# A fused bias-attention and FFN kernel: weight halves staged at most five ahead, and narrow bias groups moved to a score bank

## The chip, the cores and the metric

The kernel runs on one core of one Trainium2 chip. The metric is the device time of one execution in microseconds (us). TensorE is called PE below, VectorE DVE, ScalarE ACT, GpSimd POOL and SyncE SP, as in the profile.

## The reference

Four batches, eight heads, 576 positions, head width 64. The bias of the scores comes from a small network on a ratio of logarithms of distances, the same for every batch. Attention is followed by a layer norm and an FFN of width 2048 with a residual sum.

```python
scores = scale * np.matmul(q, k.transpose(0, 1, 3, 2))
x = (psi_rel / psi_i)[..., None]          # log1p(|i-j|) / log1p(max(i,1))
h = np.maximum(x @ w1 + b1, 0.0)          # 1 -> 32
bias = h @ w2                             # 32 -> 8 heads
scores = scores + bias.transpose(2, 0, 1)[None, :, :, :]
...
attn = attn / (np.sum(attn, axis=-1, keepdims=True) + 1e-09)
x = np.matmul(attn, v)                    # heads concatenated to (4, 576, 512)
xn = (x - mu) / np.sqrt(var + 1e-06) * g_ln
ch = np.maximum(xn @ w_ch1, 0.0) @ w_ch2  # 512 -> 2048 -> 512
return x + ch
```

The FFN weights arrive as float64 bit patterns. The kernel decodes them to float32 itself, and then splits each into two float16 parts, so that every FFN product is made of three float16 products.

## The kernel before

**Units.** A unit u is one batch, one block of 128 rows (for the last 64 rows two heads share one unit) and one head: 144 units. A Python loop over steps u writes the program. Step u holds softmax1(u) (DVE L437 adds scores and bias and finds the minimum, ACT L441 takes the exponential), the loads, softmax2(u-1), staging and decoding of weights, one group of bias rows, at odd u the two score products qk(u+1) and qk(u+2) (PE L394), the product with V (PE L483 or L512), some pieces of FFN work (PE L712 and L741), and the splitting of decoded weights. A scheduler (the tile framework's, with its own model of time) then decides in which order each engine's instructions stand. On the chip each engine works through its list in that order, and semaphores make it wait where data or a buffer are missing.

**Weights.** There are 32 raw halves n = 2f + i of 512 KB each. load_w (L613) stages a half by a DMA on SP's queue (L630), into a weight slot that is not yet needed (`fit`); the last slots, called wend, serve several halves in turn. decode_w (L637) turns it into float32 by three DVE instructions (L646, L649, L651) and gives it to PE for a Gram product (L660). The Gram products of a group of weights accumulate in the PSUM bank y1, and give the group's scale (w_scale, L663). With it split_w (L680) makes the float16 parts on ACT (L686) and DVE (L689). Only then can the FFN use the weights. How far the staging may run ahead of the decoder is this line:

```python
            if not fit or n >= len(decoded) + (6 if ustep[0] < 9 else 10):
                return False
```

**Bias groups.** The 576 rows of the bias are made in 36 groups of 16. bias_relu (L154) makes the hidden layer on DVE (L163) and ACT (L161), bias_mm (L168) multiplies on PE into a PSUM tile bps (L202 for the first 12 groups, L182 for the later ones), ACT scales it into an SBUF tile ev (L188, two instructions, one for each side of the diagonal), and a DMA writes ev to a DRAM tensor nb (L215). Later each unit loads its bias tile ldb from there (L330, L332).

**PSUM.** Score tiles sps have the tag "s" in a pool of two buffers of two banks each, which qk takes in turn. The first 12 bias groups and the one wide group (more than 512 columns) use the same two buffers. The other 23 groups use the bank y1, which is free of Gram products by then. The bank y0 collects the second FFN product (L741), and DVE adds it to x (L752).

The order of the first blocks is tails of batches 0 and 1, then block 0; the groups of block 1 are made one per step from step 28 on, those of blocks 2 and 3 every third step.

Of the kernel before, what the change touches and what calls it, by code (L numbers as in the profile page):

```python
# [8 lines left out]
F32 = mybir.dt.float32  # L9
# [13 lines left out]
def kernel(  # L23
# [33 lines left out]
    ps_s = ctx.enter_context(tc.tile_pool(name="ps_s", bufs=2, space=bass.MemoryType.PSUM))  # L57
    ps_x = ctx.enter_context(tc.tile_pool(name="ps_x", bufs=1, space=bass.MemoryType.PSUM))
    ps_h = ctx.enter_context(tc.tile_pool(name="ps_h", bufs=1, space=bass.MemoryType.PSUM))
    ps_y = ctx.enter_context(tc.tile_pool(name="ps_y", bufs=1, space=bass.MemoryType.PSUM))  # L60
# [78 lines left out]
    def after(ins, dep):  # L139
        if dep is not None:  # L140
            tc.add_manual_dep(ins.ins, dep.ins.name,
                              mybir.DependencyInfo(mybir.DependencyClass.Sync,
                                                   mybir.DependencyReason.DATA),
                              reason="pace")

    def stage(gi, name, s=0):
        if gi in gorder[0:7] and name == "r" and s % 2:
            r = ptp.tile([128, 10, 128], F16, tag="pt", name="rp")
            return r.rearrange("p a b -> p (a b)").bitcast(F32)[:, 0:EW]
        if gi in gorder[0:12] and name == "r" and gi < 35:  # L150
            return e16p.tile([128, 1152], F16, tag="e16", name="rh").bitcast(F32)
        return ep.tile([128, EW], F32, tag="e", name=name)
# [15 lines left out]
    def bias_mm(gi):  # L168
        rs, ndve = rt.pop(gi)
        nrev = 16 * gi + 16  # L170
        ntot = nrev + SEQ - 16 * gi
        n = max(SEQ - 16 * gi, nrev + 1)
        if gi in gorder[12:] and n <= 512:
            ps = ps_y.tile([128, 512], F32, tag="y1", name="bps")
        else:
            ps = ps_s.tile([128, 2, 512], F32, tag="s", name="bps")
        if gi in gorder[12:]:
            flat = ps if n <= 512 else ps.rearrange("p a b -> p (a b)")
            for a in range(0, n, 512):
                b = min(n, a + 512)  # L180
                for s in range(4):
                    T.matmul(out=flat[32 * s:32 * s + 32, a:b], lhsT=nw2_sb, rhs=rs[s][:, a:b],  # L182
                             start=True, stop=True)
            ev = stage(gi, "ev")
            cb, sc = cb_sb[:, ndve:ndve + 1], ip_sb[:, gi:gi + 1]
            for o, i in ((ev[:, 0:nrev], flat[:, 1:nrev + 1][:, ::-1]),
                         (ev[:, nrev:ntot], flat[:, 0:ntot - nrev])):
                S.activation(o, i, AF.Identity, bias=cb, scale=sc)  # L188
        else:
            hw = ntot // 2  # L190
            for hf in range(2):
                lo, up = hf * hw, min(ntot, hf * hw + hw)
                mid = min(max(nrev, lo), up)
                for a, b in ((lo, mid), (mid, up)):
                    if a == b:
                        continue
                    for s in range(4):
                        if a < nrev:
                            src = rs[s][:, nrev - b + 1:nrev - a + 1][:, ::-1]
                        else:  # L200
                            src = rs[s][:, a - nrev:b - nrev]
                        T.matmul(out=ps[32 * s:32 * s + 32, hf, a - lo:b - lo], lhsT=nw2_sb, rhs=src,  # L202
                                 start=True, stop=True)
            ev = stage(gi, "ev")
            evi[gi] = S.activation(ev[:, 0:2 * hw].rearrange("p (a b) -> p a b", a=2), ps[:, :, 0:hw],
                                   AF.Identity, bias=cb_sb[:, ndve:ndve + 1], scale=ip_sb[:, gi:gi + 1])
        c, r0 = divmod(16 * gi, 128)
        row = NH * PITCH
        dst = nflat[c][r0 * row:(r0 + 16) * row + 16]
        dst = dst.rearrange("(k x) -> k x", k=16)[:, 0:row]  # L210
        dst = dst.rearrange("k (h j) -> k h j", h=NH)[:, :, 0:ntot]
        if c == 4:
            dst = nflat[4][r0 * PITCH:r0 * PITCH + 1]
            dst = bass.AP(dst.tensor, dst.offset, [[PITCH + 1, 16], [64 * PITCH, NH], [1, ntot]])
        (G if gi in gorder[0:12] else SY).dma_start(out=dst, in_=ev[:, 0:ntot])  # L215
# [13 lines left out]
    gorder = [g for c in corder for g in range(8 * c, min(36, 8 * c + 8))]  # L229
# [378 lines left out]
    wraw, decoded = {}, set()  # L608
    ustep = [-1]
# [3 lines left out]
    def load_w():  # L613
        f, i = wload[0]
        n = 2 * f + i
        busy = {x for m, x in stg.items() if m not in decoded}
        fit = [x for x in range(NF + 1) if x not in busy and (2 * x >= n + 3 or x == 0 and n < 6)]
        if n < 2 * NF - 2:
            if not fit or n >= len(decoded) + (6 if ustep[0] < 9 else 10):
                return False  # L620
            stg[n] = fit[0]
            dst = wslot[fit[0]]
        else:
            if n >= len(decoded) + 2:
                return False
            dst = [ep.tile([128, EW], F32, tag="e", name="wst")[:, 0:512] for _ in range(2)]
        wload.pop(0)
        for j, d in enumerate(dst if isinstance(dst, list) else [dst]):
            w = d.shape[1]
            ld = SY.dma_start(out=d.bitcast(U32),  # L630
                              in_=w_ch[f].bitcast(U32)[:, 1024 * i + w * j:1024 * i + w * j + w])
            if ttri and n < 24:
                after(ld, ttri[max(ttri)])
        wraw[f, i] = dst
        return True
# [179 lines left out]
    for _ in range(4):  # L815
        load_w()
# [7 lines left out]
    for n in range(NP + 1):  # L824
        if n < NP:
            bias_relu(gorder[n], 3)
        if n > 0:
            bias_mm(gorder[n - 1])
            mm_done[0] += 1
        if n == 5:  # L830
            issue_loads(-3)
# [37 lines left out]
    while u < NU + 6 or jobs or cur_job or pend or yq:  # L869
# [15 lines left out]
        for _ in range(2):  # L885
            if wload:
                load_w()
# [6 lines left out]
        while mm_done[0] < ngroup:  # L894
            bias_mm(gorder[mm_done[0]])
            mm_done[0] += 1
# [103 lines left out]
```

## Time and profile before

| | |
|---|---|
| median of three runs | 672.0 us (669.14 to 672.3) |
| the profiled execution | 670.07 us, of which the span of its instructions is 668.3 us |
| PE busy | 640.6 us, 96% of the span |
| DVE busy | 456.5 us, 68% |
| ACT busy | 391.5 us, 59% |
| POOL busy | 95.7 us, 14% |
| mean granted TensorE clock | 0.995 of full speed |

The span runs from the first to the last instruction; 1.8 us of the profiled time lie around it. A share of busy time is a mean over the whole span: the first 120 us, in which weights are decoded, have another balance of engines than the rest, so the rows below are taken by stretches.

### The profile page before, as it was taken

The page shows a single profiled execution, that of the slowest core. Times are in us where ns is not written, and L with a number is a line of the kernel's source. Part 1 is how long each engine was busy: PE and PEld are TensorE (multiplying, and loading weights), DVE is VectorE, ACT ScalarE, POOL GpSimd, SP SyncE. Part 2 cuts the span into 40 slices and gives each one's busy share as a digit, 9 for nine tenths or more (in the row PEclk, how much of TensorE's full clock was granted, in tenths as well). Part 3 has the DMA queues.
Part 4 walks back from the last instruction along what each step waited for, and adds up shares of the span by engine and source line. Part 5 has one row for each costly group of instructions (what it writes and reads, how often), then busy time and mean ns, then how long its engine had stood idle before and what let it go on. Part 6 is the DMA issues. An engine that isn't in the chain of part 4 may idle for free. (4 is left out here: it accounts for less than half of the span.)

```text
span 668.3 us, 19124 instructions
## 1 busy us (share of the span) xinstructions
PE 640.6 (96%) x7929; PEld 447.0 (67%) x7929; DVE 456.5 (68%) x1061; ACT 391.5 (59%) x777; POOL 95.7 (14%) x163
## 2 busy tenths in 40 slices
PE   6799998998999899999899999999999999999997
PEld 4467776765566676676676666766767776777774
DVE  6699999789567577686857585657667575855321
ACT  5566755779676357888764666757544554553110
POOL 4332321001001111011101021101012110000000
PEclk9999997999999999999999999999999999999999
DMA  9999973555778997878789788789997786645100
GB/s 329 309 388 378 381 278 100 127 112 122 117 186 176 203 210 166 176 156 175 171 181 227 151 150 198 142 154 192 218 190 152 153 173 114 118 87 89 33 17 17
DMA packets 186886, 117.23 MB, mean 175 GB/s; under 512 B 163888, under 2 KB 164016, under 8 KB 186800
## 3 DMA queue, kind: packets, MB, share of 16 engines
q1 hardware_dynamic: 177056, 81.00, 55.7%
q0 software_dynamic: 9600, 34.84, 17.7%
q8 instruction: 62, 1.02, 0.6%
q10 hardware_dynamic: 144, 0.18, 0.2%
q14 instruction: 24, 0.20, 0.1%
HBM read 60.51 MB, written 15.63 MB: 114 GB/s over the span
## 5 line engine op out<-in xcount | busy, mean ns | idle before, releaser
L712 PE MATMUL hps<-xT,w 128*128 128x128 f16 x3240 | 196.2, 220 | 1.1 <-DVE hh L722 0.5
L441 ACT ACTIVATE t<-t,m 128x576 f32<-128x576 f32 x144 | 110.9, 770 | 143.2 <-DVE m L437 143.0
L741 PE MATMUL y<-w,hh 128*128 128x512 f16 x810 | 187.7, 379 | 3.6 <-DVE x L752 1.6
L712 PEld LDWEIGHTS <-w 128*128 128x128 f16 x3240 | 185.0, 98 | 6.8 <-issue 4.4
L741 PEld LDWEIGHTS <-hh 128*128 128x128 f16 x864 | 79.7, 98 | 90.2 <-ACT hh L718 3.1
L465 DVE SCALAR_TENSOR_TENSOR e<-t,e 128x512 f16<-128x512 f32 x120 | 82.8, 690 | 81.7 <-ACT e L446 81.4
L437 DVE CUSTOM_DVE_ANT_0 t<-sps,ldb 128x576 f32<-128x576 f32 x144 | 105.7, 752 | 30.7 <-PE sps L394 18.1
L394 PE MATMUL sps<-kf,qf 64*128 64x288 f32 (+1 forms) x640 | 94.7, 431 | 1.2 <-DVE m L437 0.7
L446 ACT ACTIVATE e<-t 128x576 f16<-128x576 f32 x120 | 80.8, 679 | 6.9 <-DMA wend<-e 3.3
L394 PEld LDWEIGHTS sps<-kf,qf 64*128 64x128 f32 (+1 forms) x640 | 48.0, 175 | 35.5 <-issue 19.6
L722 DVE SCALAR_TENSOR_TENSOR hh<-hps,hh 128x512 f16<-128x512 f32 x72 | 49.3, 685 | 30.2 <-ACT hh L718 29.8
L718 ACT ACTIVATE hh<-hps 128x512 f16<-128x512 f32 x72 | 41.9, 582 | 47.3 <-PE hps L712 41.8
L483 PEld LDWEIGHTS <-pt 128*128 128x128 f16 (+1 forms) x1456 | 48.6, 100 | 29.2 <-issue 24.1
L752 DVE SCALAR_TENSOR_TENSOR x<-y,ycs,x 128x512 f32<-128x512 f32 x58 | 43.3, 747 | 29.4 <-PE y L741 29.3
L483 PE MATMUL xps<-v,pt 128*128 128x64 f16 (+1 forms) x1456 | 58.1, 194 | 1.4 <-DMA pt<-e 0.6
L295 POOL DMA_DIRECT2D kf<-in_k_s_dram x56 | 31.4, 561 | 156.4 <-PE sps L394 110.3
L308 POOL DMA_DIRECT2D qf<-in_q_main_dram x32 | 18.4, 576 | 158.3 <-PE sps L394 90.4
L161 ACT ACTIVATE r<-psi_sb,par_sb 128x448 f32<-128x448 f32 (+23 forms) x72 | 39.5, 613 | 0.0
L188 ACT ACTIVATE ev<-bps,cb_sb,par_sb 128x144 f32<-128x144 f32 (+27 forms) x48 | 26.0, 592 | 22.9 <-PE bps L182 22.7
L572 POOL TENSOR_SCALAR rs<-mv 128x1 f32<-128x1 f32 x18 | 9.3, 519 | 169.4 <-DVE mv L571 161.6
L441 ACT ACTIVATION_READ_ACCUMULATOR t<-t,m 128x1 f32 x144 | 27.0, 188 | 0.0
L182 PE MATMUL bps<-r,nw_sb 128*32 128x448 f32 (+24 forms) x200 | 26.2, 494 | 0.0
(121 smaller groups left out, 636.7 us busy)
## 6 DMA issues: line engine op xcount, KB each, us to landing
kf<-in_k_s_dram POOLq DMA_DIRECT2D x56, 288.0 KB, 5.0
ldb<-nb SPq DMA_DIRECT2D x40, 288.0 KB, 4.8
w<-in_w_ch_dram SPq DMA_DIRECT2D x22, 512.0 KB, 9.3
qf<-in_q_main_dram POOLq DMA_DIRECT2D x32, 256.0 KB, 4.6
nb<-ev SPq DMA_DIRECT2D x24, 296.0 KB, 3.5
vf<-in_v_p_dram POOLq DMA_DIRECT2D x16, 320.0 KB, 9.3
wend<-in_w_ch_dram SPq DMA_DIRECT2D x8, 512.0 KB, 5.6
out_dram<-x SPq DMA_DIRECT2D x16, 256.0 KB, 2.4
```

Source lines behind the costliest of these rows:

```text
L161: S.activation(r[:, 0:n], psi_sb[:, 0:n], AF.Relu, bias=pr_sb[:, g4:g4 + 1], scale=1.0)
L394: m = T.matmul(out=o, lhsT=l, rhs=kk, start=True, stop=True, tile_position=(64 * hf, 64 * e))
L437: ttri[u] = V.tensor_tensor_reduce(out=halves(t), in0=ps[:, :, 0:HS], in1=halves(bias), scale=-0.125, scalar=3e38, op0=ALU.add, op1=ALU.mi ...
L441: S.activation(t, t, AF.Exp, bias=m, scale=-1.0, accum_out=l8[b, c][:, h:h + 1])
L446: S.activation(e16[:, 0:SEQ], t, AF.Copy, scale=E_SCALE)
L465: V.scalar_tensor_tensor(out=e16[:, 640:1152], in0=t[:, 0:512], scalar=E_SCALE, in1=e16[:, 0:512], op0=ALU.mult, op1=ALU.subtract)
L483: T.matmul(out=o, lhsT=p[:, m], rhs=v[:, j, a, :], start=(i == 0), stop=(i == len(ops) - 1))
L712: T.matmul(out=h[:, idx * n:idx * n + n], lhsT=w[:, wo + kk * 128:wo + kk * 128 + 128], rhs=xT[k][:, xo + kk, 0:n], start=(i == 0), stop=( ...
L718: S.activation(hh[:, 0], h, AF.Relu)
L722: V.scalar_tensor_tensor(out=hh[:, 1], in0=h, scalar=0.0, in1=hh[:, 0], op0=ALU.max, op1=ALU.subtract)
L741: T.matmul(out=yps[k][t], lhsT=hh[:, a, o:o + 128], rhs=w[:, wo:wo + 512], start=(f == f0 and i == 0), stop=(f == f1 - 1 and i == 2))
L752: V.scalar_tensor_tensor(out=x, in0=y, scalar=ycs[:, g:g + 1], in1=x, op0=ALU.mult, op1=ALU.add)
```

## The change

Staging may now be at most five halves ahead of the decoder, at every step. And bps of every bias group is a tile of the score pool, so the 23 narrow groups leave the bank y1 and take their turn in the two score buffers.

```diff
@@ bias_mm
-        if gi in gorder[12:] and n <= 512:
-            ps = ps_y.tile([128, 512], F32, tag="y1", name="bps")
-        else:
-            ps = ps_s.tile([128, 2, 512], F32, tag="s", name="bps")
+        ps = ps_s.tile([128, 2, 512], F32, tag="s", name="bps")
         if gi in gorder[12:]:
-            flat = ps if n <= 512 else ps.rearrange("p a b -> p (a b)")
+            flat = ps.rearrange("p a b -> p (a b)")
@@ load_w
         if n < 2 * NF - 2:
-            if not fit or n >= len(decoded) + (6 if ustep[0] < 9 else 10):
+            if not fit or n >= len(decoded) + 5:
                 return False
```

The lines below both places stand three lower in the changed kernel (L182 becomes L179, L394 L391, L630 L627, L646 L643).

SP's queue around the loads of block 0's bias tiles (ldb from nb0), before; w12 to wend are staged halves, ldb_2557 is a later bias tile of a tail:

```order
L630 DMA w11_140<-in_w_ch_dram 128x1024
L630 DMA w12_141<-in_w_ch_dram 128x1024
L630 DMA w13_142<-in_w_ch_dram 128x1024
L630 DMA w14_143<-in_w_ch_dram 128x1024
L630 DMA wend_144<-in_w_ch_dram 128x1024
L330 DMA ldb_786<-nb0_124 128x576
...
L332 DMA ldb_2557<-nb4_128 128x576
L630 DMA w10_139<-in_w_ch_dram 128x1024
L630 DMA wend_144<-in_w_ch_dram 128x1024
```

The same place with the change:

```order
L627 DMA w11_140<-in_w_ch_dram 128x1024
L627 DMA w12_141<-in_w_ch_dram 128x1024
L627 DMA w8_137<-in_w_ch_dram 128x1024
L627 DMA w9_138<-in_w_ch_dram 128x1024
L327 DMA ldb_785<-nb0_124 128x576
...
L329 DMA ldb_2557<-nb4_128 128x576
L627 DMA w10_139<-in_w_ch_dram 128x1024
L627 DMA w13_142<-in_w_ch_dram 128x1024
```

One staged half fewer (12 in place of 13) stands between the tails' bias tiles and block 0's, and the halves use other slots.

DVE from the instruction that frees the slot of half n=24 (the last reader of that slot, first row) to the first decoding instruction of that half (last row), before; t is softmax1 (L437), w11 to w13 are decoded weights, hh an FFN tile:

```order
L651 SCALAR_TENSOR_TENSOR w11_140<-wend_144,w11_140 128x512
L646 TENSOR_SCALAR w12_141<-wend_144 128x512
L651 SCALAR_TENSOR_TENSOR w11_140<-w13_142,w11_140 128x512
L437 ISA t_1562,m_1563<-sps_1492,ldb_792 128x576
...
L649 SCALAR_TENSOR_TENSOR w12_141<-w14_143,w12_141 128x512
L649 SCALAR_TENSOR_TENSOR w12_141<-wend_144,w12_141 128x512
...
L651 SCALAR_TENSOR_TENSOR w12_141<-wend_144,w12_141 128x512
...
L722 SCALAR_TENSOR_TENSOR hh_1363<-hps_1314,hh_1363 128x512
L646 TENSOR_SCALAR w13_142<-wend_144 128x512
```

The same with the change; the half is now staged in w14, whose last reader is the first row:

```order
L648 SCALAR_TENSOR_TENSOR w11_140<-w14_143,w11_140 128x512
L434 ISA t_1514,m_1515<-sps_1489,ldb_789 128x576
...
L648 SCALAR_TENSOR_TENSOR w11_140<-wend_144,w11_140 128x512
L646 SCALAR_TENSOR_TENSOR w10_139<-w12_141,w10_139 128x512
...
L648 SCALAR_TENSOR_TENSOR w12_141<-wend_144,w12_141 128x512
L686 SCALAR_TENSOR_TENSOR w4_133<-w5_134,ws_117,w4_133 128x512
...
L686 SCALAR_TENSOR_TENSOR w5_134<-w6_135,ws_117,w5_134 128x512
L643 TENSOR_SCALAR w13_142<-w14_143 128x512
```

Between release and first use stood 11 DVE instructions before, and stand 26 with the change.

PE around one of the later narrow groups that is made at an odd step, before; bps is the bias group (four matmuls), sps the scores of two units (two matmuls each), xps the product with V, hps the first FFN product:

```order
L741 MATMUL y_6576<-wend,hh 128x512
L182 MATMUL bps<-r,nw_sb 32x449 x4
L394 MATMUL sps<-kf,qf 128x288 x4
L483 LDWEIGHTS pt
L483 MATMUL xps<-v,pt 128x64
```

The same group with the change:

```order
L738 MATMUL y_6576<-wend,hh 128x512
L179 MATMUL bps<-r,nw_sb 32x449 x4
L391 MATMUL sps<-kf,qf 128x288 x2
L480 LDWEIGHTS pt
L480 MATMUL xps<-v,pt 128x64
...
L709 LDWEIGHTS w_133
L709 MATMUL hps<-xT,w_133 128x128
...
L391 MATMUL sps<-kf,qf 128x288 x2
```

The second unit's scores, which need the buffer that bps holds until ACT has copied it out, stand behind 14 matmuls of xps and 13 of hps.

## Rows read from the trace of the kernel before

**Rows 1.** Page, busy time, share of the span and instructions of the engines.

```profile
PE 640.6 (96%) x7929; PEld 447.0 (67%) x7929; DVE 456.5 (68%) x1061; ACT 391.5 (59%) x777; POOL 95.7 (14%) x163
```

**Rows 2.** Windows, four stretches: length, busy time of each engine, clock, DMA share.

```profile
core 0: us, PE busy (x) PEld busy (x) DVE busy (x) ACT busy (x) POOL busy (x), PEclk, DMA share, GB/s
...
64.00:96.00 32.00, 31.72 (x291) 25.12 (x290) 30.70 (x73) 20.50 (x51) 10.40 (x17) 1.00 0.90 333
96.00:120.00 24.00, 20.66 (x151) 14.93 (x150) 22.04 (x47) 14.88 (x30) 3.45 (x5) 0.86 0.56 150
...
150.00:180.00 30.00, 27.82 (x308) 15.97 (x304) 22.75 (x49) 24.47 (x46) 2.80 (x4) 1.00 0.55 110
...
400.00:520.00 120.00, 119.90 (x1554) 83.42 (x1552) 77.47 (x183) 71.30 (x140) 15.92 (x28) 1.00 0.89 177
```

**Rows 3.** Waits of DVE, 60 to 200 us: total, times, longest.

```profile
DVE wend L646 <- DMA wend<-in_w_ch_dram: 3.9, 1, 3.9
...
DVE t L437 <- DMA nb<-ev: 2.6, 2, 1.6
...
DVE w L646 <- DMA wend<-in_w_ch_dram: 1.2, 1, 1.2
```

**Rows 4.** Waits of PE, 60 us to the end: those for a softmax.

```profile
PE sps L394 <- DVE m L437: 0.7, 1, 0.7
```

**Rows 5.** Timeline of DVE around the decoding of half n=24.

```profile
88.48 0.67 DVE L651 SCALAR_TENSOR_TENSOR w<-wend,w 128x512 uint32<-128x512 uint32 x1
...
93.24 0.67 DVE L722 SCALAR_TENSOR_TENSOR hh<-hps,hh 128x512 f16<-128x512 f32 x1
95.15 0.43 DVE L646 TENSOR_SCALAR w<-wend 128x512 uint32<-128x512 uint32 x1 [1.23 <-DMA wend<-in_w_ch_dram]
```

**Rows 6.** Line L630, issues from 89 to 90 us, then 90 to 117 us.

```profile
DMA to landing us min/median/max: 5.9/5.9/5.9
...
DMA to landing us min/median/max: 3.7/4.7/5.9
```

**Rows 7.** Timeline of DVE, 61 to 65 us, the end of the first splits.

```profile
61.15 3.07 DVE L689 SCALAR_TENSOR_TENSOR w<-w,ws,w 128x512 f16<-128x512 f32 x4
64.25 0.76 DVE L437 CUSTOM_DVE_ANT_0 t<-sps,ldb 128x576 f32<-128x576 f32 x1
```

**Rows 8.** Timeline of PE, 100 to 103 us.

```profile
100.82 0.40 PE L660 MATMUL gram<-w 128*128 128x128 bf16 x4 [0.80 <-DVE w L651]
102.14 1.11 PE L459 MATMUL ptm<-par_sb,t 128*128 128x128 f32 x4 [0.92 <-DVE x L752]
```

**Rows 9.** Windows, the stretch of the lower clock.

```profile
101.53:108.36 6.83, 6.21 (x45) 6.00 (x46) 6.83 (x14) 3.25 (x5) 0.00 (x0) 0.50 0.00 2
```

**Rows 10.** Timeline of PE, score products of three pairs, the first pair split.

```profile
464.33 0.76 PE L394 MATMUL sps<-kf,qf 64*128 64x288 f32 x4
...
466.26 0.76 PE L394 MATMUL sps<-kf,qf 64*128 64x288 f32 x4
...
472.00 1.24 PE L394 MATMUL sps<-kf,qf 64*128 64x288 f32 x8
...
479.37 1.24 PE L394 MATMUL sps<-kf,qf 64*128 64x288 f32 x8
```

**Rows 11.** Timeline of PE, 153 to 172 us, where groups come every step.

```profile
153.47 0.58 PE L483 MATMUL xps<-v,pt 128*128 128x64 f16 x14 [0.60 <-DMA pt<-e]
...
155.15 0.91 PE L182 MATMUL bps<-r,nw_sb 128*32 128x432 f32 x2
...
160.94 0.93 PE L182 MATMUL bps<-r,nw_sb 128*32 128x432 f32 x6
163.09 0.59 PE L741 MATMUL y<-w,hh 128*128 128x512 f16 x2 [1.22 <-DVE x L752]
...
167.78 0.75 PE L394 MATMUL sps<-kf,qf 64*128 64x288 f32 x2
...
170.78 0.75 PE L394 MATMUL sps<-kf,qf 64*128 64x288 f32 x2
```

## The prediction

> **What bounds the kernel now.** I read the busy times first, then windows by stage, because the mean hides two regimes. Over the span PE is busy for 96% and DVE for 68% [rows 1]. In the windows [rows 2] the reader should compare the two columns stretch by stretch. From 64 to 96 us both are nearly full (PE 31.72 of 32.00 us, DVE 30.70). From 96 to 120 us DVE has 22.04 of 24.00 us and PE 20.66, at a mean clock of 0.86: here DVE's decoding and splitting of weights leads and PE follows. From 150 to 180 us PE has 27.82 of 30.00 and DVE 22.75, so PE leads with some gaps. From 400 to 520 us PE has 119.90 of 120.00 us. From about 113 us on, then, the end of the kernel is PE's work plus PE's gaps; anything that shifts the start of that stage carries through to the end, and anything added to PE's work in it costs its full length. DVE and ACT have slack there.
>
> Then the waits. DVE stood for a staged half twice, for 3.9 and 1.2 us, and for bias rows twice, the longer 1.6 us [rows 3]. PE stood for a softmax to free a score bank once after 60 us, for 0.7 us [rows 4].
>
> **The change part by part.** All sums are made against the profiled execution (670.07 us, of it a span of 668.3 us); the median of the three runs, 672.0 us, stands 1.9 us above it, and the sum is carried over to the median.
>
> *Staging, half n=24.* The slot of this half was freed at 88.48 + 0.67 = 89.15 us and its decoding began at 95.15, 1.23 us after the instruction at 93.24 had ended [rows 5]. The transfer, issued at 89.2 us, took 5.9 us [rows 6]. Between release and use stood 11 instructions, 4.76 us (89.15 to 93.91), 0.43 us each. With the change 26 stand between, 11.3 us at the same mean, about twice the transfer: the wait of 1.23 us goes. In the regime of 64 to 113 us DVE leads, so I take it as full: -1.2 us.
>
> *Staging, later halves.* The order also moves the release of n=27 nearer to its use: nine instructions lie between, 3.9 us at 0.43 us. Transfers of that stretch took 3.7 to 5.9 us, median 4.7 [rows 6]. So a new wait of 0 to 2.0 us; at the median +0.8 us. The half n=29 stays late (the 3.9 us of [rows 3]); one more DVE instruction of some 0.7 us now lies between, so its wait shrinks by that. PE had its own work beside most of that wait, so this is worth 0 to -0.7 us, and I take -0.35. Staging in all: -1.2 + 0.8 - 0.35 = -0.75 us.
>
> The Trainium skill, "DMA: Bandwidth & Descriptors", in the section on the anatomy of one DMA on the gpsimd path, fits a transfer by 2.0 us plus its bytes over 436 GB/s, which an estimate makes 3.2 us for 512 KB. By it n=27 would be in time and staging would bring -1.55 us; the rows here, from SP's queue, show no transfer of this stretch under 3.7 us, and the rows decide.
>
> *Staging, the queue.* One 512 KB half fewer stands ahead of block 0's bias tiles. DVE is splitting the first group of weights until 64.22 us and starts on the first of these units at 64.25 [rows 7]; an earlier bias tile has nobody waiting for it. I take 0. If that cover were gone, the gain would be about one transfer of that queue, and the range below holds it.
>
> *Bias bank, the split pairs.* A group made at an odd step sits directly ahead of a qk pair. In the bank y1 it let the pair run together. In a score buffer it takes the buffer that the pair's second unit needs, and the scheduler puts that unit's scores behind 14 xps and 13 hps matmuls, which cover the time in which ACT empties bps. The kernel before has this pattern once, for its one wide group: the scores start apart, at 464.33 and 466.26 us, and the next pair at 472.00, 7.67 us after the first; that pair is whole, and the pair behind it starts at 479.37, 7.37 us later [rows 10]. No gap stands in it; PE's work is cut into more runs. So a split costs 0.30 us. The order after the change has nine new splits where PE leads, and one split of before is gone: 8 x 0.30 = +2.4 us. From below 0 (if the runs overlap better than in that row), from above twice the row, 8 x 0.6 = +4.8.
>
> *Bias bank, pieces.* The four matmuls of a group write four different 32-row strips. One alone took 0.91 us, three together 0.93 [rows 11]: each extra piece costs about 0.9 us. The order had six extra pieces in the first dense groups before and has seven with the change: +0.9. But one group was wedged into a qk pair, which was cut into three pieces of 0.75 us (the first and last stand in [rows 11]); its new order has two pieces, at 0.76 us each as in [rows 10]: 2.25 - 1.52 = 0.7 us less. Together +0.2 us.
>
> *Bias bank, the dense stage.* Around 153 to 163 us PE stood for 0.60 and 1.22 us [rows 11], the second time for DVE, which itself had stood for bias rows. With the other order of groups these gaps may close or stay: 0 to -1.8, I take half, -0.9 us. Against this, groups then come at every step, and each is now a link in one chain of the two score buffers: softmax, bps, two evictions on ACT, next scores. Behind a late link stand on PE all later matmuls, and behind those DVE's next softmax. The price is between nothing and eight groups x 0.7 us (the one such wait that PE shows, [rows 4]) = +5.6; the only bias group before that already shared these buffers in the full stage shows no gap around it [rows 10], so I take one wait, +0.7.
>
> The sum: -0.75 + 2.4 + 0.2 - 0.9 + 0.7 = +1.65 us, 671.7 us for the profiled execution and **673.6 us** for the median. All lower bounds together would be -1.2 - 0.7 + 0 + 0.2 - 1.8 = -3.5 us, all upper ones -1.2 + 2.0 + 4.8 + 0.2 + 5.6 = +11.4 us; the upper bounds of the splits and of the chain of buffers are the unlikeliest of them.
>
> **The rivals.** A measurement of this kernel cannot tell less than about 0.5% (3.4 us) from no change; I use this bound for the three chances.
>
> *Forecast, within 0.5%: 0.58.* Small terms of both signs, 668.6 to 675.4 us.
>
> *Slower, the low clock on PE's own time: 0.14.* After the gaps of 0.80 and 0.92 us at 100 and 102 us [rows 8], the granted clock was 0.50, which is 1.2 GHz, for 6.83 us (101.53 to 108.36), and DVE was busy for all of it [rows 9]: the drop was covered. The gaps move with DVE's order. Once the drop falls behind 113 us, where PE leads, half of it is lost: 3.4 us on top of the sum, 677.0 us. Against it: the gaps stay in the same phase of decoding. The point that decides is whether a stretch below 1.00 reaches past 113 us.
>
> *Slower, the chain of score buffers: 0.15.* If four of the eight dense groups or more cost the 0.7 us of [rows 4], in place of one, the sum passes +3.4 us; all eight give 673.6 + 4.9 = 678.5 us. For it: both buffers are taken at every step there, and PE has 2.2 us of gaps in 150 to 180 us already [rows 2]. Against it: the split order puts work between.
>
> The Trainium skill, "TensorE: Matmul & The Clock Gate", section "A second HAM failure mode: psum-queue depth-cycling", says that cycling through PSUM banks lets PE idle briefly between groups, often enough that its clock falls and rises. By it the dense stage would also show a low clock; the trace before, which cycles two score buffers throughout, is at 1.00 in both of the later windows [rows 2], so of the 0.15 above it gets 0.02, at one drop of 3.4 us, 677.0 us.
>
> *Faster, the lead of DVE carried whole: 0.13.* Were the two waits for halves gone with no new one, the gaps of [rows 8] closed (1.7 us) and with them the drop of the clock, the dense gaps closed too (1.8), and the splits free, the time would be 672.0 - 1.2 - 0.7 - 1.7 - 1.8 = 666.6 us. DVE's 22.04 of 24.00 us between 96 and 120 [rows 2] bounds it: DVE can give at most 2 us there. It decides if the splits cost under 0.1 us each.
>
> *One part does nothing: inside the forecast.* If the limit of five changed no wait, the time would be 674.35 us; if the splits were free, 671.2 us.
>
> **How the numbers follow.** The likeliest case gives 673.6 us. Faster has 0.13, within 0.5% 0.58, slower 0.14 + 0.15 = 0.29. The range leaves out about one in ten on each side: below, most of the faster case, so 668.5; above, the worst half of the chain of buffers, so 677.5.
>
> **What would show it.** In the profile of the changed kernel: the wait of 1.2 us for wend at n=24 is missing in DVE's waits, a wait under 1 us for n=27 may stand in its place, and that for n=29 is near 3.1 us. Split pairs appear as two runs of four score records with 14 xps and 13 hps between, and the spacing to the next pair is 7.67 us where it was 7.37; PE's busy time in 210 us to the end is larger by about 2 us. The stretch of the lower clock ends before 113 us. In 150 to 210 us PE's waits on DVE's softmax (scores and bps) and on ACT's eviction come to less than 1 us in all. The prediction is wrong if those waits exceed 3 us, if a split costs much more or less than 0.3 us, or if PE reaches the steady stage more than 3 us earlier or later than before.

## The result, and the profile after

The changed kernel takes 679.82 us (median of 18 runs, 671.6 to 684.9), the kernel before 670.97 us beside it (18 runs, 665.27 to 676.38). The ratio is 1.011, 95% interval 1.0074 to 1.0146 (disturbed executions are left out of ratios, so it is not the quotient of the medians): slower, and beyond the upper end of the forecast's range. The profiled execution takes 678.17 us with a span of 676.4 us, 8.1 us more than the span before. Of these 8.1 us, PE's busy time accounts for 4.4 (against [rows 1]) and its idle time for the rest:

```profile
PE 645.0 (95%) x7929; PEld 446.0 (66%) x7929; DVE 456.8 (68%) x1061; ACT 393.2 (58%) x777; POOL 95.4 (14%) x163
```

To find the place in this execution, I cut both spans at two points that mean the same in each: where PE starts the product with V of unit 28 and of unit 40. Windows of the kernel before (columns as in [rows 2]):

```profile
0.00:60.00 60.00, 47.97 (x661) 31.44 (x662) 46.98 (x123) 36.25 (x67) 20.03 (x39) 1.00 0.95 352
60.00:153.47 93.47, 87.75 (x822) 67.38 (x819) 85.67 (x201) 64.01 (x137) 20.12 (x31) 0.96 0.68 206
153.47:228.01 74.54, 71.70 (x838) 45.13 (x838) 48.27 (x108) 51.29 (x101) 5.77 (x11) 1.00 0.78 156
228.01:668.30 440.29, 433.19 (x5612) 303.01 (x5612) 275.62 (x631) 239.97 (x475) 49.76 (x82) 1.00 0.72 148
```

The same stretches of the changed kernel:

```profile
0.00:60.00 60.00, 48.64 (x657) 32.02 (x658) 46.71 (x122) 36.94 (x67) 20.11 (x39) 0.97 0.95 347
60.00:154.14 94.14, 85.44 (x826) 64.68 (x823) 88.26 (x206) 66.67 (x141) 19.80 (x31) 1.00 0.66 210
154.14:235.16 81.02, 74.08 (x838) 46.15 (x838) 45.69 (x104) 48.21 (x95) 5.86 (x11) 0.96 0.77 146
235.16:676.40 441.24, 436.80 (x5612) 303.18 (x5612) 276.12 (x631) 241.35 (x475) 49.65 (x82) 1.00 0.73 147
```

Third rows: the same 838 matmuls take 81.02 us instead of 74.54, 6.5 of the 8.1 us. Idle time there is 6.94 us instead of 2.84, and busy time is 2.38 us more at a mean clock of 0.96. The stretch ahead gives 0.7 us, the 440 us behind only 0.95.

The waits of PE for transposed softmax tiles name the idle time. Before, 40 us to the end (total, times, longest):

```profile
PE xps L483 <- DMA wend<-e: 1.3, 1, 1.3
...
PE xps L483 <- DMA pt<-e: 0.6, 1, 0.6
```

After:

```profile
PE xps L480 <- DMA wend<-e: 5.4, 1, 5.4
PE xps L480 <- DMA pt<-e: 4.7, 3, 3.1
```

From 1.9 to 10.1 us. These transposes (softmax2, L473 before, L470 after) turn the float16 exponentials of a unit by a DMA on SP's queue into a tile of the pool pt, or, for every fifth unit from 35 on, into the weight slot wend. The two long waits in PE's timeline after:

```profile
154.14 0.93 PE L480 MATMUL xps<-v,pt 128*128 128x64 f16 x14 [3.14 <-DMA pt<-e]
...
235.16 0.96 PE L480 MATMUL xps<-v,wend 128*64 128x64 f16 x28 [5.37 <-DMA wend<-e]
```

The first is unit 28 (its row before is in [rows 11], with a wait of 0.60), the second unit 40. Around both the granted clock was half, 1.2 GHz; windows after:

```profile
154.01:157.42 3.41, 3.28 (x39) 3.29 (x40) 2.73 (x4) 2.64 (x5) 0.00 (x0) 0.50 0.27 74
232.52:239.34 6.82, 4.18 (x36) 2.01 (x37) 3.34 (x8) 2.61 (x5) 0.78 (x2) 0.50 1.15 202
```

Before, the one such stretch after 60 us lay at 101.53 to 108.36 [rows 9], in the stage that DVE sets.

**Why unit 40's tile is late.** When the last bias rows of block 1 reach DRAM, SP is released, issues the waiting bias tiles of block 1 and then the transposes of units 40 and 41. SP's timeline before:

```profile
214.92 1.29 SPq L330 DMA_DIRECT2D ldb<-nb  x3
216.37 1.26 SPq L473 DMA_TRANSPOSE wend<-e  x1
217.80 5.58 SPq L473 DMA_TRANSPOSE pt<-e  x1
```

After:

```profile
216.55 2.41 SPq L327 DMA_DIRECT2D ldb<-nb  x4
219.13 2.21 SPq L470 DMA_TRANSPOSE wend<-e  x1
221.50 4.71 SPq L470 DMA_TRANSPOSE pt<-e  x1
```

In the same microseconds POOL issues its own copies of keys and queries; POOL's timeline after:

```profile
219.39 0.54 POOL L292 DMA_DIRECT2D kf<-in_k_s_dram  x1 [5.49 <-PE sps L391]
219.94 0.54 POOL L305 DMA_DIRECT2D qf<-in_q_main_dram  x1
220.47 0.54 POOL L292 DMA_DIRECT2D kf<-in_k_s_dram  x1
```

Both queues' packets run on the core's 16 DMA engines: from 219 to 236 us of after, SP's took 68.7% of the engines' time and POOL's 41.6%. The time from issue to landing of the three transposes there, before and then after:

```profile
DMA to landing us min/median/max: 8.3/11.6/12.6
```

```profile
DMA to landing us min/median/max: 10.7/14.5/16.0
```

Unit 28's transpose, with the engines to itself, took 3.2 us in the kernel before. So the collision was there before, too: its 1.3 us wait was its visible tip. In the profiled execution after the change it is longer, and PE asks 5.4 us before it is over.

### The profile page after: what moved, and what is told of

It reads as the page before. It is cut to its first block, busy times and chain, and to the rows that moved or that the text cites. A ratio compares the mean times of both kernels' runs of the same rounds, so it can differ in the third digit from the quotient of the medians.

```text
span 676.4 us, 19136 instructions
## 1 busy us (share of the span) xinstructions
PE 645.0 (95%) x7929; PEld 446.0 (66%) x7929; DVE 456.8 (68%) x1061; ACT 393.2 (58%) x777; POOL 95.4 (14%) x163
## 4 chain that ended last, share of the span: by engine, by line
PE 61%; DMA 3%; ACT 1%; DVE 1%; issue 0%; DVEq 0%; ACTq 0%
PE hps L709 22%; PE y L738 22%; PE sps L391 8%; PE xps L480 7%; DMA wend<-e 2%; PE bps L179 2%; DMA nb<-ev 1%; ACT v L366 0%; ACT t L438 0%; ACT e L443 0%; ACT r L161 0%; DVE v L369 0%; DVE hh L719 0%; DVE t L434 0%; DVE x L749 0%
## 5 line engine op out<-in xcount | busy, mean ns | idle before, releaser
L738 PE MATMUL y<-w,hh 128*128 128x512 f16 x810 | 189.6, 382 | 0.2 <-ACT hh L715 0.2
L391 PE MATMUL sps<-kf,qf 64*128 64x288 f32 (+1 forms) x640 | 96.7, 436 | 0.7 <-DVE m L434 0.7
L391 PEld LDWEIGHTS sps<-kf,qf 64*128 64x128 f32 (+1 forms) x640 | 47.5, 176 | 33.8 <-issue 17.4
L179 PE MATMUL bps<-r,nw_sb 128*32 128x448 f32 (+24 forms) x200 | 26.8, 494 | 0.0
```

The costliest lines, as they stand in the source:

```text
L391: m = T.matmul(out=o, lhsT=l, rhs=kk, start=True, stop=True, tile_position=(64 * hf, 64 * e))
L738: T.matmul(out=yps[k][t], lhsT=hh[:, a, o:o + 128], rhs=w[:, wo:wo + 512], start=(f == f0 and i == 0), stop=(f == f1 - 1 and i == 2))
```

## The experiments

Each was run in five rounds beside the kernel before on the same chip; ratios are to that kernel. Where nothing else is said, an edit is made in the changed kernel, called "after" from here on.

**The changed kernel once more, and its two halves.** r1_after_again is unchanged. r2_stage_only has only the new limit (first diff, against the kernel before); r3_bank_only only the score bank (second diff, against after):

```diff
-            if not fit or n >= len(decoded) + (6 if ustep[0] < 9 else 10):
+            if not fit or n >= len(decoded) + 5:
```

```diff
-            if not fit or n >= len(decoded) + 5:
+            if not fit or n >= len(decoded) + (6 if ustep[0] < 9 else 10):
```

> The changed kernel once more, to see which of its waits come back. Theory A (transposes landing late: PE waits for the probabilities' transposes at about 151 and 230 us, and its clock falls behind each): ratio to before 1.009 to 1.014, PE's waits of xps for DMA 8 us or more again (10.1 in the first profile), two stretches at 0.50 clock in PE's own stage. Theory B (the split score pairs are the loss): the same ratio, but PE's busy time from 260 us to the end grows by 5 us or more, and the waits may differ from the first profile.

> Only the staging limit of five; bias groups stay in the bank y1. SP has, as in the kernel before, three of block 1's bias tiles ahead of the first transpose into wend. Theory A: the wait at about 230 us stays near that of before (1 to 2 us), the one at 151 us may remain (0.5 to 3 us) because the order of the tails' transposes is that of the change: ratio 0.998 to 1.005. Theory B: no split pairs, so 0.996 to 1.000.

> Only the move of bps to the score buffers; the staging limit stays 6 and 10. SP has four of block 1's bias tiles ahead of the first transpose into wend, as with the whole change. Theory A: a wait of 3 to 6 us at about 230 us and a clock drop behind it, ratio 1.007 to 1.012. Theory B: no such wait needed; eight splits at 0.3 us give 1.003 to 1.005, and the excess of the whole change needs both parts.

r1: median 678.49 us, ratio 1.0086 (1.005 to 1.0122). Its profiled execution was one of the quicker (span 671.7 us). PE waited 5.4 us for transposes there, where 8 or more were expected: the waits for pt tiles came back (4.6 us), that for unit 40 was 0.8, and no half clock followed them. So the length of the collision differs from execution to execution, while the loss of the whole set came again. A stretch of half clock lay in PE's own stage, but at another place; window of r1:

```profile
114.99:118.41 3.42, 3.42 (x10) 1.24 (x9) 2.58 (x5) 1.20 (x3) 0.00 (x0) 0.50 1.28 267
```

How much of the loss goes with the clock can be read from the executions that enter the ratios. Of the changed kernel's 14 there, eight had a mean clock of 0.990 or more and took 673.7 us in median; the other six (0.982 to 0.985) took 678.9 to 681.5. In r1 it was five of nine at 674.2, the rest 677.9 to 679.5. Of the kernel before beside r1, 29 of 33 were at 0.990 or more, at 670.05, and none under 0.987. At a like clock, then, the change costs about 4 us; the rest of the 5.8 to 7.4 us that the ratios make comes with the lower clock.

r2: 1.0087 (1.0049 to 1.0126), above what either theory gave it. r3: 1.0013 (0.9984 to 1.0041), below both of its forecasts. The loss is the staging's. PE's waits from 140 to 260 us in r2:

```profile
PE xps L483 <- DMA pt<-e: 3.0, 1, 3.0
PE xps L483 <- DMA wend<-e: 2.7, 1, 2.7
```

and in r3, where the same four bias tiles stand ahead of unit 40's transpose but the three transposes there landed after 8.0 to 10.1 us:

```profile
PE xps L483 <- DMA pt<-e: 1.2, 2, 0.6
```

**Taking the collision apart from two sides.** r4_ldb_spread holds back SP's bias tiles of block 1; r5_kq_hold leaves SP alone and makes POOL's two key copies wait until unit 41's transpose has landed (first and second diff; the second one's first two lines stand behind the loads of keys and of queries):

```diff
-            if need > u + LOOK[kind]:
+            if need > u + (4 if kind == "b" and key[1] == 1 else LOOK[kind]):
...
-                    SY.dma_start(out=raw, in_=nbias[c][:, h, :])
+                    ld = SY.dma_start(out=raw, in_=nbias[c][:, h, :])
+                    if c == 1:
+                        after(ld, ttri[max(ttri)])
```

```diff
+                if 50 <= u <= 60:
+                    after(ld, tins[41])
...
-        SY.dma_start_transpose(out=p, in_=e16)
+        tins[u] = SY.dma_start_transpose(out=p, in_=e16)
```

> The whole change, and block 1's bias tiles are each held back until the softmax of a step at most four units before their use, so that they leave SP's queue two at a time behind the transposes instead of four at once ahead of one. PE's order is almost that of the whole change, splits included. Theory A: PE's wait of 5.4 us at 230 us falls under 1.5 us, no low clock there, the time falls by 5 to 7 us to a ratio of 1.000 to 1.005. Theory B: within 1.5 us of the whole change.

> The whole change, and two loads of keys (kf, on POOL's queue) that otherwise start beside the transposes of units 40 and 41 wait until the second of these transposes has landed. The order on PE, SP, DVE and ACT is that of the whole change, with the same four bias tiles ahead of the first transpose. Theory A1 (the transposes are slow because POOL's copies share the DMA engines with them): they take under 9 us where they took 16.0 and 14.5, PE's wait there falls under 1.5 us, ratio 1.000 to 1.005. Theory A2 (they are late because they queue behind four bias tiles on SP): the wait stays at 3 us or more, ratio 1.007 to 1.012.

r4: 1.002 (0.9991 to 1.0048). r5: 1.0015 (0.9985 to 1.0044). Landing of the transposes at that place in r4, and then in r5:

```profile
DMA to landing us min/median/max: 3.4/5.3/5.6
```

```profile
DMA to landing us min/median/max: 3.3/4.5/5.8
```

Both edits remove the wait for unit 40 altogether; neither kernel has any wait of PE from 200 to 260 us. r5 leaves SP's order as it was, so POOL's key copies are needed for the delay. r4 leaves POOL alone, but is the weaker test: without the tiles ahead of it unit 40's transpose also leaves SP 3.9 us earlier (215.2 us against 219.1). The volume moved shows the delay as well. DMA view of after, 219 to 236 us (packets, volume, mean; then issues with median time to landing):

```profile
DMA packets 3141, 2.57 MB, mean 151 GB/s; under 512 B 2467, under 2 KB 2467, under 8 KB 3140
...
kf<-in_k_s_dram POOLq DMA_DIRECT2D x2, 288.0 KB, 13.5
```

and of r5, 217 to 230 us:

```profile
DMA packets 5366, 3.00 MB, mean 231 GB/s; under 512 B 4640, under 2 KB 4640, under 8 KB 5364
...
kf<-in_k_s_dram POOLq DMA_DIRECT2D x2, 288.0 KB, 5.1
```

So in after the copies are slowed with the transposes. But being in flight together is not enough. In r4 the same three copies, issued from 219.4 us, ran beside transposes issued at 218.2 and 222.3 us, and all were quick; DMA view of r4, 214 to 226 us:

```profile
kf<-in_k_s_dram POOLq DMA_DIRECT2D x2, 288.0 KB, 4.6
...
pt<-e SPq DMA_TRANSPOSE x3, 4.6
```

What else the slow case needs, the bias tiles ahead or a start within the same microsecond, was not separated.

**The same hold on the other versions.** r6_before_spread is the kernel before with r4's hold, r7_bank_spread r3 with it, r10_stage_spread r2 with it, r11_before_both the kernel before with the holds of r4 and r5.

> The kernel before, with block 1's bias tiles held back as in the spread run, and nothing else. Theory A: the burst cost the kernel before something too (1.3 us of wait and what follows from it), so 1 to 4 us less than before, ratio 0.994 to 0.999. Theory B: 0.999 to 1.001.

> The move of bps to the score buffers, with the staging limits of before and block 1's bias tiles held back. Against the same hold without the move (the run beside it) this prices the split pairs alone: 0.3 us each for seven or eight gives +2 to +2.5 us, a ratio of 0.996 to 1.002.

> The whole staging limit of five, bias groups in y1, and block 1's bias tiles held back. Theory A: without the crowd of transfers at 220 us the staging limit keeps only what it loses at the tails' transposes (a 3 us wait at about 151 us and a clock drop, less the 2 us gained in decoding): 2 to 4 us above the kernel before with the same hold, ratio 0.999 to 1.003, against 1.0087 without the hold. Theory B (the staging loss sits in DVE's decoding and does not depend on the transfers at 220 us): 1.005 or more.

> The kernel before with both holds: block 1's bias tiles and the two loads of keys that start at about 220 us. If the bias tiles' hold alone already clears the transposes, nothing more is gained: 0.995 to 0.999, as with the one hold. If POOL's copies still slow them, 0.992 to 0.995.

| | without the hold | with it |
|---|---|---|
| kernel before | 1 | r6 0.9967 (0.9935 to 0.9998) |
| bank only | r3 1.0013 (0.9984 to 1.0041) | r7 0.9982 (0.9954 to 1.001) |
| limit only | r2 1.0087 (1.0049 to 1.0126) | r10 1.0045 (1.0013 to 1.0078) |
| both (after) | 1.011 and 1.0086 | r4 1.002 (0.9991 to 1.0048) |

Every row falls: by r6 the kernel before was paying about 0.33% or 2.2 us for the collision; the changed kernel pays 0.7 to 0.95%, 4.4 to 6.4 us (1.0086 to 1.002, and 1.011 to 1.0015). r6 is the version that beats both kernels, if by little; r11, with the second hold on top, gained nothing more (0.999, 0.9961 to 1.0019), so a gain of 0.3% is near the limit of what these runs resolve. The right column still has the limit of five on the slow side: 1.002 against 0.9967 is 0.53% or 3.6 us, with about 0.4% of uncertainty. The collision is not the whole loss. Bank against no bank there is 0.9982 to 0.9967, 1.0 us, which is inside the uncertainty. The row of the limit alone says it most plainly: the limit costs 0.87% without the hold and, r10 against r6, 0.78% or 5.2 us with it. There the hold gives back no more than it gives the kernel before, and r10 (1.0045) lies between the forecasts of both its theories. Its trace has no wait for unit 40, but 10.24 us of half clock:

```profile
124.67:134.91 10.24, 10.24 (x63) 8.27 (x64) 7.14 (x22) 6.59 (x16) 1.63 (x2) 0.50 0.26 59
```

**Which half of the limit.** r8_lim_early5 has five before step 9 and ten later, r9_lim_late5 six and then five, both are made in the kernel before:

```diff
-            if not fit or n >= len(decoded) + (6 if ustep[0] < 9 else 10):
+            if not fit or n >= len(decoded) + (5 if ustep[0] < 9 else 10):
```

```diff
-            if not fit or n >= len(decoded) + (6 if ustep[0] < 9 else 10):
+            if not fit or n >= len(decoded) + (6 if ustep[0] < 9 else 5):
```

> Only the early half of the staging limit: five in place of six before step 9, ten kept behind it, bias groups in y1. Its order on SP is that of the staging change up to the bias tiles of block 1. If the early half alone shifts the transposes of the tails, PE's wait of about 3 us at 150 to 160 us and the late lag of 3 us or more at unit 44 come back, ratio 1.004 to 1.011; if the later limit (10 to 5) is what counts, 0.997 to 1.002.

> Only the later half of the staging limit: five in place of ten from step 9 on, six kept ahead of it, bias groups in y1. The order on SP around the tails' transposes and block 1's bias tiles is that of before. If the early half is what shifts the transposes, this stays at 0.997 to 1.003 with PE's waits on transposes at 2 us or less; if any delay of staging does it, 1.004 or more.

r8: 1.0053 (1.0019 to 1.0087), with waits of 2.9 and 2.8 us for units 28 and 40. r9: 1.0023 (0.9992 to 1.0055), with 2.9 us for unit 28, where at most 2 were expected, none for unit 40, and half clock from 35.5 to 42.3 and from 107.2 to 114.0 us. The early half costs something clear of the noise; whether the late one costs at all is undecided.

**Unit 28.** What is left in r4 and r5 is the first long wait, 3.0 us for unit 28, with half the clock behind it. SP cannot issue this transpose until its pt tile is free; the wait stands on SP as a semaphore row, which names count, ns and start. After:

```profile
L470 SPq EVENT_SEMAPHORE  x1: 1926/1926/1926, 147.1 to 147.1; - x1
L470 SPq DMA_TRANSPOSE pt<-e x1: 1293/1293/1293, 149.1 to 149.1; - x1
...
DMA to landing us min/median/max: 5.0/5.0/5.0
```

PE gets to this product at 151.00 us (154.14 less its wait of 3.14); in the kernel before it got there at 152.87 (153.47 less 0.60, [rows 11]). The 1.87 us are what this execution had gained up to there. The transpose, too, was issued 1.1 us earlier (149.1 against 150.2 us), but it landed after 5.0 us in place of 3.2, so the tile came at 154.1 us, later than before (153.4). An early PE is not what it takes: in r1, r2, r9 and r10 PE got to this product only at 154.8 to 157.1 us, and still waited 2.9 to 3.0 us.

The long landing stands beside an instruction fetch (queue q8 of the DMA view), one packet of 16 KB. In after it runs from 152.06 to 152.98 us; the last two packets of unit 28's transpose, 4 bytes each, start only as it ends. DMA views of after, 152.00 to 152.95 and 152.96 to 153.20 us:

```profile
DMA packets 5, 0.02 MB, mean 18 GB/s; under 512 B 4, under 2 KB 4, under 8 KB 4
...
q8 instruction: 1, 0.02, 6.1%
```

```profile
DMA packets 2, 0.00 MB, mean 0 GB/s; under 512 B 2, under 2 KB 2, under 8 KB 2
```

The packets of the other traces show the same in all eight in which PE waits 2.9 us or more for unit 28 (after, r1, r2, r4, r5, r8, r9, r10): the last packets start 3.6 to 4.0 us after the issue, at or just behind the end of the fetch, and the transpose lands after 4.8 to 5.0 us. In the six others (before, r3, r6, r7, r11, r12) all packets have started by 2.8 us, and it lands after 3.2. In r3, r6, r7 and r11 the fetch also starts before that, at about 2.6 us, so its nearness alone does not decide.

r12_t28_free is r5 with a place of its own for this one tile:

```diff
+        elif u in (28,):
+            p = ep.tile([128, EW], F32, tag="e", name="pe").bitcast(F16)[:, 0:1152].rearrange("p (a b) -> p a b", b=128)
```

> The whole change with the hold of the two key loads, and the transposed probabilities of unit 28 go to a spare tile of another pool, so that their transpose need not wait until PE has multiplied unit 24's; the order on the engines differs in some 20 places of the stage from 145 to 205 us. Theory A (behind the first collision the rest of the staging loss is this one transpose: it starts late, PE waits 3 us for it at 151 us and then runs 3.4 us at half clock): the wait falls under 1.5 us, no low clock at 154 us, 2 to 4 us less than with the hold alone (0.995 to 0.999 of before). Theory C (the rest is the order of the dense groups behind it): within 1.5 us of the hold alone (1.0015).

r12: 1.0018 (0.9982 to 1.0053). All waits for transposes are gone from its profile, but the ratio is r5's, outside what theory A gave. Windows of r12 say where the gain went:

```profile
120.00:150.00 30.00, 28.75 (x216) 22.31 (x216) 21.66 (x57) 17.95 (x37) 3.30 (x5) 0.77 0.29 67
150.00:180.00 30.00, 28.99 (x353) 18.89 (x351) 24.10 (x52) 25.74 (x49) 2.45 (x4) 1.00 0.51 108
```

The row of 150 to 180 us has 28.99 us of PE's work, where r5 has 25.83. In the row ahead of it the clock was half from 122.46 to 136.11 us, while PE was busy for 13.55 of 13.65 us; at its start PE's timeline has a gap:

```profile
122.56 0.61 PE L663 MATMUL gram<-wend 128*128 128x128 bf16 x4 [1.25 <-DVE wend L654]
```

r5 has 0.74 us at that place and kept the clock there in its profile. Ten of r5's twelve executions had a mean clock of 0.992 or more, against two of r12's. Those two were at 0.997 and took 665.27 and 665.91 us; the others (0.983 to 0.990) took 669.92 to 674.98. r5's executions at 0.995, on another chip, took 670.2 to 671.1. So freeing unit 28's tile is worth some 5 us where the clock holds, by these few executions, and in most the clock takes it back. Why it falls after this gap so much more often in r12 is open; r12's unit 28 comes later than the gap, so it cannot be the cause by itself.

## Why the prediction was wrong, point by point

**Right.** The wait at n = 24 is gone and n = 29 waits 3.1 us, as forecast. DVE's waits for staged halves after, 60 to 130 us, are this single row:

```profile
DVE wend L643 <- DMA wend<-in_w_ch_dram: 3.1, 1, 3.1
```

A split pair costs 0.30 us: in PE's timeline after, the next pair starts 7.67 us after the first half of a newly split one, against 7.37 for a whole pair [rows 10]. Six of the seven new splits behind 270 us have this spacing, the seventh 8.33.

```profile
423.67 0.76 PE L391 MATMUL sps<-kf,qf 64*128 64x288 f32 x4
...
425.60 0.76 PE L391 MATMUL sps<-kf,qf 64*128 64x288 f32 x4
...
431.34 1.24 PE L391 MATMUL sps<-kf,qf 64*128 64x288 f32 x8
```

The chain of score buffers, a rival at 0.15, did not come: PE's waits from 140 to 260 us hold nothing of that kind in after or in r3. The bank part measured +0.9 us (r3) and +1.0 us (r7 against r6) for the +2.4 us that its four terms sum to, inside their uncertainty. The second failure mode of the clock from the Trainium skill, "TensorE: Matmul & The Clock Gate", section "A second HAM failure mode: psum-queue depth-cycling", had 0.02; r3, whose groups do cycle through the score buffers, has a mean clock of 0.994 against 0.995 before, and 1.00 from 150 to 210 us, so no run here shows it. One of the prediction's own signs of being wrong came: PE reached unit 40, in the stage that it sets, 7.15 us later than before, where 3 was the bound. So did the sign of the rival on the clock, a stretch of half clock past 113 us.

**Wrong size.** The later half n = 27 had +0.8 us and shows no wait. Of the dense stage's -0.9, the row at 163.09 [rows 11] did vanish, but the wait for unit 28 grew by more.

**The step that failed** is the staging taken as a matter of the decoder alone: "*Staging, the queue* ... I take 0", beside "anything that shifts the start of that stage carries through to the end". The limit alone, summed at -0.75 us, measured +5.8 us (r2). In the profiled execution a start 1.87 us earlier did not carry through: unit 28's product met a transpose that landed 1.8 us more slowly, waited 3.14 us instead of 0.60, and started 0.67 us later than before (154.14 against 153.47). At 220 us the transfers met in another order of time, and 12 us of collision became 16; why they were that much slower is not shown. The trace before had both signs, the idle row at 153.47 in [rows 11] with 0.60 us and the 1.3 us at unit 40; I counted the first among gaps that "may close" and left the second out. A wait of 0.6 us for a DMA said that this product was bound by the transfer and not by PE, so an earlier arrival there was worth no more than an earlier landing.

In terms of the sum: with the collision removed the changed kernel stands at +0.15 to +0.2% (r4, r5), 1.0 to 1.3 us over the kernel before, where the sum said +1.65. That agreement is partly luck, since by r6 the kernel before gains 2.2 us by the same hold. The terms left out are 2.2 to 4.2 us of collision (4.4 to 6.4 less the 2.2 that the kernel before pays too) and, by the trace, about 2.4 us at unit 28: the start 0.67 us later, and 1.7 us lost in the 3.41 us of half clock behind it. What can be tested of this is that 2.4 + 1.0 us for the bank stands against the 3.6 us between r6 and r4. It is not proven: the uncertainty there is some 3 us, r12 took unit 28's wait away and gained nothing in the median, and in the kernel with the limit alone the collision's extra is only 0.6 us (0.87% less 0.78%). How the loss divides between transposes and clock is open; that the limit makes it is not.

**The rival of the low clock**, at 0.14, came true in part, and further than the trace of after shows. Stretches at 0.50 did come to lie on PE's own time, as the windows show. In the trace of after they follow or surround the waits for transposes, and none stands just behind 113 us, where the rival put it. But r1, the same kernel, has one at 114.99 us, r2 one of 6.83 us from 123.46, r10 and r12 those shown above, all with PE busy throughout or nearly so; the kernel before and r3 and r6 have theirs end by 114.3 us. So its place was right for some executions. Its price of 3.4 us also falls short of the whole loss, about 4 us of which is there at a like clock.

## What to carry to other kernels

A short wait for a DMA on the engine that sets the end (0.6 and 1.3 us here) means that the transfer has no slack: before pricing a change upstream at "shifts carry through", follow each such transfer to what releases its issue and to what shares the DMA engines with it. Freeing a few microseconds in an early stage moves all later bursts against one another; a burst of prefetches that is released by one event belongs behind the transfers that the critical engine asks for next, which here took a hold of a few lines and gave 0.3%, as far as these runs resolve it. A gap closed on PE is only gained if the clock does not fall at the next one.

## What the runs showed of the hardware

Transposes and copies in flight together can slow each other far more than their volume says: behind four bias tiles and beside three copies, 10.7 to 16.0 us for a transpose of 288 KB that takes 3.2 us alone, at a mean of 151 GB/s, against 231 GB/s and 3.3 to 5.8 us where the key copies came after. They need not: in r4 the same three copies beside transposes left both at 3.4 to 5.6 us. The Trainium skill, "DMA: Bandwidth & Descriptors", section "Queues, rings and completion order", says that each DMA engine goes round between the queues it has work for, a packet at a time, and that a transfer's signal lands only after every earlier write of that engine, across its queues. Both fit that r5, which only held back another queue's copies, brought the transposes back; how much each of the two does, no run here shows.

Unit 28's transpose landed after 4.8 to 5.0 us in eight traces and after 3.2 us in six, with no copies between its packets. In the eight an instruction fetch of 16 KB stands ahead of its last 4-byte packets, which start when the fetch ends or up to 0.3 us behind it; that accounts for about 1 of the 1.7 us. No run moved the fetch.

The granted clock fell to half in stretches of 3.41 to 13.65 us, at other places in different executions of one kernel. Those behind 100 us begin around or within 2 us behind gaps of PE, some of several us (5.37 in after), some as short as 0.65 us (r1, ahead of 114.99). Those of the changed kernel at a mean clock of 0.990 to 0.995 took 671.6 to 678.2 us, those at 0.977 to 0.985 678.9 to 684.9 us.
